# Attention sums into an ELU layer on one core: a later place for z in the head, and two 128-row stores at the end

## The chip, the cores and the metric

The kernel runs on one core of one Trainium2 chip. The metric is the device time of one execution in microseconds (us); the kernel before takes 267.29 us (median of 3 runs, 267.2 to 267.3). Less is better. Engines are named as in the profile: PE is TensorE (PEld its weight loads), DVE is VectorE, ACT is ScalarE, POOL is GpSimd, SP is SyncE, whose only work here is to issue transfers (DMAs); ACT can issue transfers too.

## The reference

What is computed, cut to what matters:

```python
batch, n_heads, seq, head_dim, r = 4, 4, 1088, 32, 8       # x: 4352 tokens x 128; w_in 128 x 2048, w_out 2048 x 128
def phi(x):                                   # 32 features -> 64
    a = einsum('rd,bhsd->bhsr', S1, x)
    b = einsum('rd,bhsd->bhsr', S2, x)
    return einsum('bhsi,bhsj->bhsij', a, b).reshape(..., r * r)
q_p, k_p = phi(q), phi(k)
kv  = einsum('bhsf,bhsd->bhfd', k_p, v)
z   = sum(k_p, axis=2)
num = einsum('bhsf,bhfd->bhsd', q_p, kv)
den = einsum('bhsf,bhf->bhs', q_p, z)[..., None] + 1e-06
x   = (num / den).transpose(0, 2, 1, 3).reshape(4352, 128)
h   = x @ w_in
g   = where(h > 0, h, exp(minimum(h, 0)) - 1)
out = g @ w_out
```

The arrays are given in 64-bit floats, so the weights are turned into 32-bit floats on the chip (the functions RA, RB and RC, some five instructions for each block of weights, most of them on DVE).

## The kernel before, in words

The sequence is cut into 68 half tiles of 64 tokens (17 for each of 4 batches); a token of batch b, place y and half tile t is row (b, y, t) of the output, so neighbouring rows of one half tile lie 17 output rows apart (`NT = 17`), and half tile t+2 lies two rows behind half tile t. Nine query groups `g` hold up to 8 half tiles each; the last, `g = 8`, holds four.

The order of work is written out by hand: the order of the calls is the order of each engine's queue, and engines wait for each other only where data asks for it. There are three stages.

**The head** (to about 22 us). For batch 0: DVE transposes the keys (`transp(kT, ...)`, L244), `KF(0)` multiplies them with the sketch matrices on PE (tile `abp`, L304) and ACT copies the result out of PSUM in two pieces (`abk`, L312). Two things are made of these key features:
- z, the sums for the denominator. `Z_first` gives PE 9 small products (`zps`, L382, 18 instructions), ACT copies their result (`zl`, L404), `Z` multiplies it with a mask matrix on PE (`zps`, L226, 4 instructions) and `Z_out` writes z into `SW` on DVE (L413). `q1z_first` multiplies the queries with it on PE (`zqp`, L491).
- the products of the features, `kp`: `KO_pool` makes the first four tiles of nine on POOL (L287), `KO_first(t0, t1)` the tiles t0 to t1 on DVE (L374, out of PSUM). `KA(0)` sums them with v on PE (`kv`, L391).

`q1_first` does for the queries what `KF` does for the keys (`abqp`, L479, copied by ACT to `abq`, L483); it needs the transposed queries (`qT`, L244). `q2_den` makes the quotient on DVE: `pw` (L566) from `abq` and `zqp`, then `den`, `an`, and `q2_out` the query features `qp` (L583). Behind it on DVE come the roundings of the first weights and the second query group; the first `mm2` (tile `o`, L226) follows them. `keep_warm(n, cols)` gives PE n products of cols columns whose result nobody reads (`idle`, L231).

**The middle.** For each group and each 256-wide block of w_in: `h` on PE, two ACT passes (L788, L790), one DVE pass (L796), and the second product on PE (`o`, or `pa` and `pb`, L727).

**The end.** The last group ends in `mm2_last`, which leaves two PSUM tiles of 128 tokens x 128 features, each of two half tiles (`ol`, i = 0 and 1; output half tiles 64+i in partitions 0 to 63 and 66+i in partitions 64 to 127). `fin_last` copies tile 0 by ACT and tile 1 by DVE (L840) and stores each tile as two transfers of 64 rows, one issued by SP and one by ACT (L843).

Of the kernel before, what the change touches and what calls it, by code (L numbers as in the profile page):

```python
# [22 lines left out]
def _ap(ap: bass.AP, free):  # L23
    return dataclasses.replace(ap, ap=[list(ap.ap[0])] + [list(x) for x in free])
# [3 lines left out]
def kernel(  # L28
# [21 lines left out]
    nc = tc.nc  # L50
# [8 lines left out]
    KT = (NT + 1) // 2  # L59
# [164 lines left out]
    def halves(dst, lhs, rhs, **kw):  # L224
        for u in range(2):
            nc.tensor.matmul(dst[64 * u:64 * u + 64], lhs[:, 64 * u:64 * u + 64], rhs, skip_group_check=True,  # L226
                             tile_position=(0, 64 * u), **kw)

    def keep_warm(n, cols=256):
        for i in range(n):  # L230
            nc.tensor.matmul(idle[:, :cols], some[:, :P], some[:, :cols], skip_group_check=True)  # L231
# [11 lines left out]
    def transp(dst, x, b, t0, t1):  # L243
        nc.vector.transpose(dst[b][:, t0:t1, :].rearrange("p t (a c) -> p c t a", c=2), hd[x, b][:, :, t0:t1, :])  # L244
# [124 lines left out]
    def KO_first(t0, t1):  # L369
        half, o = divmod(t0, 5)  # L370
        n = t1 - t0
        a_ = kf_ps[half][:, 64 * o:64 * (o + n)].rearrange("p (m x r) -> p m x r", x=2, r=R)[:, :, 1, :]
        b_ = feats[0][:, 0, t0:t1].rearrange("p t h r -> p (t h) r")
        nc.vector.tensor_mul(feats[0, half][:, o:o + n].rearrange("p t h i j -> p (t h) i j"),  # L374
                             _ap(a_, list(a_.ap[1:]) + [[0, R]]), _ap(b_, [[R, n * H], [0, R], [1, R]]))
# [3 lines left out]
    def z_tile(b, ps, i):  # L379
        c = 32 * (i % 4)  # L380
        ab = feats[b]
        nc.tensor.matmul(ps[c:c + 32, R * R:R * R + H * R], ab[:, 0, i].rearrange("p h r -> p (h r)"),  # L382
                         ab[:, 1, i].rearrange("p h r -> p (h r)"), start=(b == 0 and i < 4), stop=(i >= KT - 4),
                         skip_group_check=True, tile_position=(0, c))
# [17 lines left out]
    def ZC(b, ps):  # L402
        zl = work.tile([P, H * R], F32, name="zl", tag="zl")
        nc.scalar.copy(zl[:], ps[:, R * R:R * R + H * R])  # L404
        return zl

    def Z(b, ps, zl):

        halves(ps[:, 96:128], SXh[:], zl[:])

    def Z_out(b, ps):
        z = wzs[b] = SW[:, :, 2, :] if b == 0 else work.tile([FD, H, R], F32, name="wz", tag="wz")[:]
        nc.vector.tensor_mul(z, ps[:, 96:128].rearrange("p (h i) -> p h i", h=H), _ap(bmask[:], [[1, H], [0, R]]))  # L413
# [21 lines left out]
    def Z_first():  # L435
        ps = psum.tile([P, 512], F32, name="zps", tag="h", bufs=4)
        for i in range(KT):
            z_tile(0, ps, i)
        return ps, ZC(0, ps)

    def KS_first():
        kd = work.tile([P, 2, R * R], F32, name="kd", tag="kd", bufs=1)
# [18 lines left out]
    def half_tile(g, k):  # L461
        return divmod(8 * g + k, NT)
# [11 lines left out]
    def q1_first():  # L474
        p = psum.tile([P, 512], F32, name="abqp", tag="aux")
        for i in range(4):
            for u in range(2):
                b, t = half_tile(0, 2 * i + u)
                nc.tensor.matmul(p[64 * u:64 * u + 64, i * 64:i * 64 + 64], qT[b][:, t, :],  # L479
                                 Sab[:].rearrange("p h y -> p (h y)"),  # L480
                                 skip_group_check=True, tile_position=(0, 64 * u))
        abw[0] = work.tile([P, H * 4, 2 * R], F32, name="abq", tag="abq", bufs=1)
        nc.scalar.copy(abw[0][:].rearrange("p (h t) y -> p h t y", h=H),  # L483
                       p[:, :256].rearrange("p (t h y) -> p h t y", t=4, h=H))

    def q1z_first():
        p = psum.tile([P, 512], F32, name="zqp", tag="h", bufs=4)
        for i in range(4):
            for u in range(2):
                b, t = half_tile(0, 2 * i + u)  # L490
                nc.tensor.matmul(p[64 * u:64 * u + 64, i * 32:i * 32 + 32].rearrange("p (h r) -> p h r", h=H),  # L491
                                 qT[b][:, t, :], SW[:, :, 2, :], skip_group_check=True, tile_position=(0, 64 * u))
        return p[:, :128].rearrange("p (t h r) -> p h t r", t=4, h=H)
# [341 lines left out]
    def fin_last():  # L835
        g, n = NQ - 1, qn[NQ - 1]
        o = work.tile([P, 2, P], F32, name="ol", tag="ol", bufs=1)
        rows = out.rearrange("(b y t) f -> b y t f", b=B, t=NT)
        for i, copy in enumerate((nc.scalar.copy, nc.vector.tensor_copy)):
            copy(o[:, i, :], ops[g][i][:])  # L840
            for u, eng in enumerate((nc.sync, nc.scalar)):
                b, t = half_tile(g, u * n + i)
                eng.dma_start(rows[b, :, t, :], o[64 * u:64 * u + 64, i])  # L843


    for t0, t1 in ((0, 5), (KT, KT + 5), (5, KT), (KT + 5, NT)):
        transp(kT, "k", 0, t0, t1)
    KF(0)
    transp(qT, "q", 0, 0, 8)
    zps, zl = Z_first()  # L850
    q1_first()
    KO_pool()
    KO_first(4, 5)
    KO_first(5, 7)
    Z(0, zps, zl)
    Z_out(0, zps)
    KO_first(7, KT)
    keep_warm(1, 96)
    zq = q1z_first()
    RA(0)  # L860
    q2_den(0, zq)
# [132 lines left out]
    for n in range(2, N + 2):  # L994
        if n < N:
            g, cp = steps[n]
# [26 lines left out]
        g, cp = steps[n - 2]  # L1023
# [5 lines left out]
        elif n > 2:  # L1029
            mm2(g, cp, cp == 0, cp == NP - 1)  # L1030
            if cp == NP - 1:
                fin1(g)
    fin_last()


# [27 lines left out]
```

## Time and profile before

| | |
|---|---|
| median of 3 runs | 267.29 us (267.2 to 267.3) |
| the profiled execution, its own time | 267.2 us |
| its span, first to last instruction | 265.4 us |
| granted TensorE clock, mean | 0.998 |
| PE busy | 259.6 us (98%) |
| DVE busy | 187.5 us (71%) |
| ACT busy | 184.1 us (69%) |
| POOL busy | 159.9 us (60%) |
| mean traffic of the transfers | 51 GB/s |

The profile is of one execution. Between the span and that execution's own time lie 1.8 us which are not in the trace. In lines of instructions the first number is the start in us from the begin of the span, the second the time from the start of the first to the end of the last of the instructions that the line holds; "xN" is how many there are, and the bracket says how long the engine was idle before and for whom it waited. Times of DMA-issuing instructions (SPq, ACTq) are those of the issue; the data moves later.

### The profile page before, as it was taken

Reading aid. Unit: us, or ns where it says so; the run is one execution under the profiler, and the core shown is the slowest. Engines: PE = TensorE matmul, PEld = TensorE weight load, DVE = VectorE, ACT = ScalarE, POOL = GpSimd, SP = SyncE. Lnnn points to the kernel's source line nnn. Section 1 sums busy time; section 2 is a strip of 40 time slices with the busy share of each in tenths; the row PEclk is TensorE's granted clock in tenths of the full one; section 3 lists DMA queues with packets and bytes.
Section 4 is the critical chain, followed back from the end, with each engine's and each line's share of the span. In section 5 each row is a group of like instructions: output and inputs, shape, how many; then the busy total and the mean of one; then the engine's idle time right before and its main releaser. Section 6 shows DMA issues by size and latency. Waiting matters only on the chain.

```text
span 265.4 us, 7688 instructions
## 1 busy us (share of the span) xinstructions
PE 259.6 (98%) x3115; PEld 154.4 (58%) x3115; DVE 187.5 (71%) x347; ACT 184.1 (69%) x355; POOL 159.9 (60%) x233
## 2 busy tenths in 40 slices
PE   8999999999999999999999999999999999999994
PEld 6752323343334665667666666666766666666884
DVE  6899999996969796996557776654346444673652
ACT  2479978667567566785577777777777777777782
POOL 4400009104316985798859799898688888898300
PEclk9999999999999999999999999999999999999999
DMA  5999960020002200001100110001001100010011
GB/s 191 324 347 260 264 177 4 0 67 22 0 0 38 48 4 0 2 3 20 27 2 0 23 21 2 0 13 24 11 0 18 28 1 0 14 16 15 2 28 34
DMA packets 26418, 13.60 MB, mean 51 GB/s; under 512 B 19216, under 2 KB 24592, under 8 KB 26384
## 3 DMA queue, kind: packets, MB, share of 16 engines
q1 hardware_dynamic: 25792, 12.66, 18.7%
q8 instruction: 24, 0.39, 0.6%
q10 hardware_dynamic: 592, 0.46, 0.5%
q14 instruction: 10, 0.08, 0.1%
HBM read 10.88 MB, written 2.23 MB: 49 GB/s over the span
## 4 chain that ended last, share of the span: by engine, by line
PE 93%; DVE 5%; issue 1%; ACT 0%; DVEq 0%
PE h L226 43%; PE pb L727 16%; PE pa L727 12%; PE o L226 11%; PE ol L226 3%; PE kv L391 1%; PE idle L231 1%; PE h L645 1%; PE qps L645 1%; DVE qp L583 1%; PE kfps L323 1%; PE qps L539 1%; PE abp L304 1%; PE kv L226 1%; DVE raw L121 0%
## 5 line engine op out<-in xcount | busy, mean ns | idle before, releaser
L796 DVE SCALAR_TENSOR_TENSOR gg<-e,h 128x512 f32<-128x512 f32 (+1 forms) x144 | 92.2, 652 | 64.1 <-ACT e L790 62.8
L226 PE MATMUL h<-xg,W 128*64 128x512 f32 (+1 forms) x584 | 128.7, 563 | 0.0
L788 ACT ACTIVATE e<-h 128x512 f32<-128x512 f32 (+1 forms) x144 | 81.5, 566 | 50.4 <-PE h L226 47.9
L790 ACT ACTIVATE e<-e 128x512 f32<-128x512 f32 (+1 forms) x144 | 87.5, 607 | 4.4
L226 PEld LDWEIGHTS h<-xg,W 128*64 128x64 f32 x584 | 40.1, 137 | 47.4 <-issue 36.8
L707 POOL TENSOR_TENSOR tt<-gg 128x256 f32<-128x256 f32 x48 | 35.2, 733 | 16.3 <-DVE gg L796 15.9
L710 POOL TENSOR_TENSOR tt<-gg 128x256 f32<-128x256 f32 x48 | 35.4, 738 | 14.2 <-DVE gg L796 13.8
L712 POOL TENSOR_TENSOR tt<-gg,tt 128x256 f32<-128x256 f32 x48 | 36.6, 762 | 3.8
L711 POOL TENSOR_TENSOR tt<-tt,gg 128x256 f32<-128x256 f32 x48 | 35.2, 734 | 3.8
L727 PEld LDWEIGHTS pa<-gg,W 128*64 128x64 f32 x384 | 23.6, 137 | 22.7 <-issue 22.0
L226 PE MATMUL o<-gg,W 128*64 128x512 f32 x128 | 30.5, 597 | 0.4 <-DVE W L129 0.4
L727 PE MATMUL pa<-gg,W 128*64 128x128 f32 x384 | 29.5, 274 | 0.0
L727 PE MATMUL pb<-tt,SS 128*64 128x128 f32 x384 | 29.1, 273 | 0.0
L727 PEld LDWEIGHTS pb<-tt,SS 128*64 128x64 f32 x384 | 22.6, 137 | 0.0
L126 POOL TENSOR_TENSOR raw<-raw,tiny 128x512 f32<-128x512 f32 x1 | 1.0, 1046 | 29.7 <-DVE raw L121 29.7
L727 PE MATMUL pb<-gg,SS 128*64 128x128 f32 x192 | 18.7, 273 | 0.0
L727 PE MATMUL pb<-tt,W 128*64 128x128 f32 x192 | 18.7, 273 | 0.0
L727 PE MATMUL pa<-tt,SS 128*64 128x128 f32 x192 | 18.7, 273 | 0.0
L226 PEld LDWEIGHTS o<-gg,W 128*64 128x64 f32 x128 | 8.5, 136 | 16.2 <-issue 13.8
L727 PEld LDWEIGHTS pa<-tt,SS 128*64 128x64 f32 x192 | 12.1, 137 | 0.0
L727 PEld LDWEIGHTS pb<-tt,W 128*64 128x64 f32 x192 | 12.1, 137 | 0.0
L727 PEld LDWEIGHTS pb<-gg,SS 128*64 128x64 f32 x192 | 12.1, 137 | 0.0
(150 smaller groups left out, 243.8 us busy)
## 6 DMA issues: line engine op xcount, KB each, us to landing
raw<-in_moe_w_in_dram SPq DMA_DIRECT2D x8, 256.0 KB, 5.8
raw<-in_moe_w_out_dram SPq DMA_DIRECT2D x8, 256.0 KB, 6.0
hd_k<-in_k_dram SPq DMA_DIRECT2D x3, 544.0 KB, 7.6
hd_q<-in_q_dram SPq DMA_DIRECT2D x3, 544.0 KB, 3.2
v<-in_v_dram SPq DMA_DIRECT2D x4, 288.0 KB, 6.5
out_dram<-ob SPq DMA_DIRECT2D x72, 16.0 KB, 1.5
v<-in_v_dram SPq DMA_DIRECT2D x4, 256.0 KB, 7.5
out_dram<-ob SPq DMA_DIRECT2D x16, 32.0 KB, 1.7
```

Source lines behind the costliest of these rows:

```text
L226: nc.tensor.matmul(dst[64 * u:64 * u + 64], lhs[:, 64 * u:64 * u + 64], rhs, skip_group_check=True, tile_position=(0, 64 * u), **kw)
L231: nc.tensor.matmul(idle[:, :cols], some[:, :P], some[:, :cols], skip_group_check=True)
L304: nc.tensor.matmul(ps[i // 5][64 * u:64 * u + 64, 64 * (i % 5):64 * (i % 5) + 64], kT[b][:, u * KT + i, :], Sab[:].rearrange("p h y -> p ( ...
L645: nc.tensor.matmul(ps[w][s * r:s * r + s, 64 * k:64 * (k + m)], lhs, qpT[g, i][rows, o + 2 * k:o + 2 * (k + m), f, :], start=(f == 0 and j ...
L707: nc.gpsimd.tensor_tensor(t[:, 0], b12, b11, op=SUB)
L710: nc.gpsimd.tensor_tensor(t[:, 2], b22, b12, op=SUB)
L711: nc.gpsimd.tensor_tensor(t[:, 1], t[:, 2], b11, op=ADD)
L712: nc.gpsimd.tensor_tensor(t[:, 3], b21, t[:, 1], op=SUB)
L727: nc.tensor.matmul(bank[64 * u:64 * u + 64, P * col:P * col + P], lhs, rhs[:, u], start=(first and i in (0, 3)), stop=last, skip_group_che ...
L788: nc.scalar.activation(e, hs[g, cp][c][:, :n], RELU, scale=-1.0)
L790: nc.scalar.activation(e, e, EXP, scale=-1.0)
L796: nc.vector.scalar_tensor_tensor(gs[g, cp][:, c, :n], es[g, cp][:, c, :n], -1.0, hs[g, cp][c][:, :n], op0=ADD, op1=MAX)
```

## The change

Two places are changed. In the head, all of z's steps (the sums, ACT's copy, the mask product, `Z_out` and the filling product on PE) become one function that is called behind `q1_first`, `KO_pool` and all of `KO_first`; `KO_first` for the tiles 5 to 8 becomes one instruction in place of two; the filling product has 160 columns in place of 96. At the end, each of the two last tiles is stored by one transfer of 128 rows, the first issued by ACT, the second by SP.

```diff
@@ Z_first
         for i in range(KT):
             z_tile(0, ps, i)
-        return ps, ZC(0, ps)
+        zl = ZC(0, ps)
+        Z(0, ps, zl)
+        Z_out(0, ps)
+        keep_warm(1, 160)
@@ fin_last
-        for i, copy in enumerate((nc.scalar.copy, nc.vector.tensor_copy)):
+        for i, (copy, eng) in enumerate(((nc.scalar.copy, nc.scalar), (nc.vector.tensor_copy, nc.sync))):
             copy(o[:, i, :], ops[g][i][:])
-            for u, eng in enumerate((nc.sync, nc.scalar)):
-                b, t = half_tile(g, u * n + i)
-                eng.dma_start(rows[b, :, t, :], o[64 * u:64 * u + 64, i])
+            b, t = half_tile(g, i)
+            eng.dma_start(rows[b, :, t:t + n + 1:n, :].rearrange("y u f -> u y f"), o[:, i])
@@ the head's calls
     KF(0)
     transp(qT, "q", 0, 0, 8)
-    zps, zl = Z_first()
     q1_first()
     KO_pool()
     KO_first(4, 5)
-    KO_first(5, 7)
-    Z(0, zps, zl)
-    Z_out(0, zps)
-    KO_first(7, KT)
-    keep_warm(1, 96)
+    KO_first(5, KT)
+    Z_first()
     zq = q1z_first()
```

In the new store `n` is 2. The side in SBUF is 128 partitions of 128 elements. The side in DRAM is written as (u, y, f): two groups u of 64 rows y of 128 elements f; u steps by 2 output rows, y by 17.

## The prediction

> **What bounds the kernel now.** I read the page first, then the chain of waits, the timeline of the head and of the end, and the traffic of single transfers. The page:
>
> ```profile
> span 265.4 us, 7688 instructions
> PE 259.6 (98%) x3115; PEld 154.4 (58%) x3115; DVE 187.5 (71%) x347; ACT 184.1 (69%) x355; POOL 159.9 (60%) x233
> GB/s 191 324 347 260 264 177 4 0 67 22 0 0 38 48 4 0 2 3 20 27 2 0 23 21 2 0 13 24 11 0 18 28 1 0 14 16 15 2 28 34
> ```
>
> PE is busy for 98%, but that is a mean over stages. The chain of waits (start, length, what) shows who carries the head:
>
> ```profile
> 8.07 0.61 PE abqp L479 x16
> 8.69 0.11 PE zps L226 x4
> ...
> 8.90 0.19 DVE SW L413
> 9.09 0.60 DVE kp L374
> ...
> 9.92 0.30 DVE pw L566
> ...
> 11.26 1.29 DVE qp L583 x2
> ...
> 21.30 0.44 DVE W L129
> 21.73 0.04 issue
> 21.78 1.94 PE o L226 x8
> ```
>
> From 8.90 to 21.73 every step is one of DVE, with gaps of issue alone. From 21.78 on PE runs to 261.91 with no pause that counts. So DVE time lost or won ahead of 21.73 reaches the end in full: PE's `o` waits for DVE's last weight rounding, and nothing between them has slack. DVE has one idle stretch after 7.5 us, ahead of SW (timeline: start, length, what, and in brackets the idle time before it):
>
> ```profile
> 7.47 1.00 DVE L374 TENSOR_TENSOR kp<-abp,abk 128x256 f32<-128x256 f32 x2
> ...
> 8.14 0.19 ACT L404 COPY zl<-zps 128x32 f32<-128x32 f32 x1 [0.39 <-PE zps L382]
> ...
> 8.74 0.37 ACT L483 COPY abq<-abqp 128x256 f32<-128x256 f32 x1 [0.41 <-PE abqp L479]
> 8.90 0.19 DVE L413 TENSOR_TENSOR SW<-zps,bmask 128x32 f32<-128x32 f32 x1 [0.42 <-PE zps L226]
> ```
>
> The end is a row of steps behind the last matmul: copy, issue, packets, landing.
>
> ```profile
> 261.79 1.20 SPq L843 DMA_DIRECT2D out_dram<-ol  x2
> 261.79 1.19 ACTq L843 DMA_DIRECT2D out_dram<-ol  x2
> 261.93 0.29 DVE L840 COPY ol<-ol 128x128 f32<-128x128 f32 x1 [1.04 <-PE ol L226]
> ```
>
> Each issue takes 0.55; the second pair leaves at 262.44. By the traffic of this window the first packet starts 1.21 after the first issue (263.00) and the last ends at 264.05; 1.37 more pass to the end of the span (265.42).
>
> **The head, step by step.** Removed: one start of an instruction (two pieces of `KO_first` are joined). Moved: z's steps, past `q1_first` on PE, past the `abq` copy on ACT, past POOL's products (z gives POOL no instruction there, and no transfer moves) and past one `KO_first` piece on DVE. New times:
> - `q1_first` now waits for `qT` alone. That ends at 7.55 (6.84 + 0.71); DVE to PE takes 0.05 (SW ends 9.09, `zqp` starts 9.14). It takes 0.69: 7.60 to 8.29.
> - ACT copies `abq` first: 8.34 to 8.71 (0.05 behind PE as now, 0.37 long).
> - PE does z's 18 pieces behind `q1_first`. The parts of 8 and 10 pieces took 0.27 and 0.31, mostly drain, so 18 end at about 8.6, under the `abq` copy: nothing.
> - `zl` 0.19 on ACT: 8.71 to 8.90. It was under `q1_first` before; now it is on the path.
> - mask product: 0.05 hand-over and 0.26: ends 9.21. To DVE 0.12 (8.78 to 8.90 now): SW 9.33 to 9.52.
> - `zqp`: 0.05 + 0.66: ends 10.23; to DVE 0.12: `pw` at 10.35.
>
> `pw` starts at 9.92 now: **+0.43 us**. On DVE the joined `KO_first` (0.68 + 0.60 now; joining saves some 0.08) ends by 9.1, ahead of SW, and the rounding RA (0.28) lies between SW and `pw`; both fill waiting, so neither counts. Behind the waiting SW on DVE stand RA, and behind that ACT's RB; behind the later `pw` stands the whole DVE chain to 21.73. KA on PE starts 0.4 later too and its result is needed no earlier than before, relative to DVE. The filling product costs nothing while SW's wait covers it: 64 more columns, twice, at 0.86 ns (256 columns in 0.22 at 11.53) are 0.11; that puts its end about 0.1 ahead of `zqp`; with that cover gone it costs up to 0.1. Bounds: 0.3 (`zl` overlapping the copy ahead of it by 0.1, as ACT's neighbours elsewhere do) to 0.6 (z's pieces 0.1 later, the filling product uncovered). What is late next is PE's `o` at 22.2, and by it all the rest.
>
> **The end, step by step.** Two issues of 0.55 fall away, one on each queue. SP no longer has a first store: its only one goes when DVE's copy ends (262.22, so 262.25 in place of 262.44), a gain of 0.19. The trace has no 128-row issue of this form: 0.33 (a 128-row weight load on SP) to 0.74 (a load on ACT); I take 0.55, nearest in form. Nothing is queued behind it but the end of the program.
>
> What counts is how the packets spread. The traffic from 1.68 to 1.82, where the two 8-row loads of the sketch matrices pass (queue q1 is SP's, q10 ACT's; packets, MB, share of 16 engines):
>
> ```profile
> q10 hardware_dynamic: 16, 0.00, 9.0%
> q1 hardware_dynamic: 16, 0.00, 8.6%
> ```
>
> from 252.6 to 253.0, one store of 128 runs over 32 partitions:
>
> ```profile
> q1 hardware_dynamic: 144, 0.02, 26.2%
> ```
>
> and from 262.5 on, the last four stores:
>
> ```profile
> q10 hardware_dynamic: 160, 0.07, 10.0%
> q1 hardware_dynamic: 160, 0.07, 8.1%
> ```
>
> A load of 8 rows makes 16 packets: 8 of data and 8 of 4 bytes. A store of 64 rows makes 80 (64 + 16; each queue has two), the one of the middle 144 (128 + 16). So each engine that a transfer uses adds one small packet, and an outermost count of 8 gets 8 engines where 64 or 32 get 16. And the two 8-row loads, from SP and ACT, share their engines: packet by packet, ACT's start some 20 ns behind SP's (1.703 and 1.723, 1.705 and 1.726, 1.707 and 1.731).
>
> The new store counts 128 outermost in SBUF, but 2 in DRAM: u steps 2 rows, y 17, so they don't fold. I take the smaller count to decide, as 8 did: 2 engines, 64 rows each, the same 2 for both stores. That is 128 packets of 512 B on each of them; now each of 16 gets 16 (8 for each pair of stores). The page's best slice, 347 GB/s, is 21.7 per engine: 23.6 ns a packet (the stores' own packets follow each other by 23.5 and are recorded with 27). 128 x 23.6 ns = 3.02 us from ACT's first packet at 263.00: 266.02 in place of 264.05, **+1.97 us**. SP's earlier issue is then worth nothing, since its packets join a queue. Bounds: 16 engines, -0.2 (SP's 0.19; with the issue at 0.33, -0.4); at 30 ns a packet (the stores' engine time, 52.3% of 16 x 0.5 us in the window from 263.6, less the small ones, over 128) +2.85. The nearest row is the 8-row load, the only one with few outer rows, so I take +1.97.
>
> The Trainium skill speaks both ways. "DMA: Bandwidth & Descriptors", section on rules for kernel authors, says that two transfers to disjoint partition halves share the same engines anyway and advises one 128-partition transfer; by this alone the end would be about -0.2. The same page, section "Why a DMA increments its semaphore by 16 and not by 1", says that the engines used are the largest number up to 16 that divides the slowest dimension of both sides: 2 here; by it the end is +1.97. The packets of the 8-row loads fit the second; no row here has two sides with different outer counts.
>
> **Sum.** 267.2 (the profiled execution: span 265.4 and 1.8 around it) + 0.43 + 1.97 = **269.6 us**. The median is 267.29, 0.1 above that execution, within this rounding.
>
> **The rivals.**
> 1. *The rows spread over 16 engines* (the SBUF side's 128 decides). Then packets take 0.42 as now, the end gives 0.2 back, and only the head is left: 267.2 + 0.43 - 0.2 = 267.4, not slower by what can be told. For it: all stores in the trace use 16. Against: all of these have 32 or more outer rows on both sides. It decides from 8 engines on: both stores are then 32 packets on each engine, 0.75, done by 263.9, ahead of now; on 4 engines 64 packets take 1.51, to 264.51, and the sum is 268.1.
> 2. *Two engines for each store, but not the same two.* SP's packets start at 263.46 (262.25 + 1.21) and take 64 x 23.6 = 1.51: 264.97, +0.92, so 268.55. Against it: the pairwise packets of the 8-row loads.
> 3. *Two engines that write slower than the mean rate*, at 30 ns or more a packet: 267.2 + 0.43 + 2.85 = 270.5. For it: some stores' packets took 40 to 50 ns when SP and ACT wrote together.
> A gain in the head would need SW ahead of 8.90, but `zl` can't start before 8.6 and SW comes 0.6 behind it.
>
> **How the numbers follow.** Forecast 0.70 (own range 269.1 to 270.2: the head's 0.3 to 0.6, 23.6 to 27 ns a packet, the first packet up to 0.2 earlier with a short issue), rival 1 0.18, rival 2 0.06, rival 3 0.06. The forecast and rivals 2 and 3 leave 0.18 and their own tails out, so the range reaches down to rival 1's middle, 267.4, and up to rival 3's, 270.6. Within 0.2% (0.53 us, about what a measurement of this kernel can tell from no change): most of rival 1, 0.14. Slower: the rest, 0.84. Faster by more: 0.02.
>
> **What would show it.** Right: SW near 9.3 after a wait for `zps`, `pw` near 10.35 after a second wait, for `zqp`, and PE's first `o` near 22.2; 130 packets for each last store (128 + 2), traffic at some 43 GB/s for about 3 us, and a span near 267.8. Wrong in the end: 144 packets in a burst of 0.4 us. Wrong in the head: `o` at 21.8 or earlier.

## The result, and the profile after

The changed kernel takes 270.37 us (median of 6 runs, 269.95 to 270.84); the kernel before took 267.51 us in the runs beside it (6 runs, 267.2 to 268.47). The ratio is 1.0103, 95% interval 1.0081 to 1.0124: slower by 1%. The forecast was 269.6 us, in a range from 267.4 to 270.6; 270.37 lies near the upper end of it. The profiled execution took 270.53 us with a span of 268.7; before it was 267.2 with 265.4.

The chain of waits of the changed kernel, in its head (start, length, what):

```profile
2.07 5.25 DMA hd_q<-in_q_dram
7.32 0.02 issue
7.34 0.72 DVE qT L244
8.06 0.14 issue
8.20 0.70 PE abqp L482 x16
8.92 0.37 ACT abq L486
9.29 0.13 ACT zl L404
9.43 0.14 issue
9.56 0.31 PE zps L226 x4
9.87 0.47 PE idle L231 x2
10.34 0.61 PE zqp L494 x16
10.95 0.02 issue
10.98 0.30 DVE pw L569
...
22.38 0.44 DVE W L129
22.82 0.04 issue
22.86 1.94 PE o L226 x8
```

Read it from below. PE's first `o` starts at 22.86 where it started at 21.78: 1.08 us later. `pw` is 1.06 later (10.98 for 9.92), so the DVE chain between them hands the delay on whole. And the chain now runs back through the queries (`abqp`, `abq`, `qT`) to the load of q; before, it ran back through z's sums to the key features. The waits of DVE in the first 23 us (in total, times, longest) say the same:

```profile
DVE qT L244 <- DMA hd_q<-in_q_dram: 0.9, 1, 0.9
...
DVE pw L569 <- PE zqp L494: 0.6, 1, 0.6
DVE SW L413 <- PE zps L226: 0.5, 1, 0.5
```

and in the profile before:

```profile
DVE SW L413 <- PE zps L226: 0.4, 1, 0.4
...
DVE qT L244 <- DMA hd_q<-in_q_dram: 0.2, 1, 0.2
```

There are two waits for z's chain, SW's and `pw`'s, where there was one of 0.4. The wait for the q load was 0.2 and is 0.9: q landed later in this execution, by 0.50 at the end of `qT` (8.05 for 7.55). Its transfers were issued at the same times as before, to 0.02 us, and none of the moved steps runs ahead of it.

The end, by the timeline and by the traffic from 262.5 us on (40 slices of GB/s; then packets, MB and share of 16 engines for ACT's and SP's queue):

```profile
262.87 0.66 ACTq L845 DMA_DIRECT2D out_dram<-ol  x1
263.01 0.29 DVE L843 COPY ol<-ol 128x128 f32<-128x128 f32 x1 [1.04 <-PE ol L226]
263.33 0.63 SPq L845 DMA_DIRECT2D out_dram<-ol  x1
```

```profile
GB/s 0 0 0 0 0 0 0 0 0 0 13 20 30 40 46 43 26 40 26 43 43 46 40 43 46 43 43 43 43 43 46 40 0 0 0 0 0 0 0 0
...
q10 hardware_dynamic: 130, 0.07, 4.0%
q1 hardware_dynamic: 130, 0.07, 3.5%
```

The same row of the profile before, also from 262.5 us on:

```profile
GB/s 0 0 0 0 0 0 28 92 233 297 184 64 7 0 0 28 113 170 262 234 92 7 0 0 0 0 0 0 0 0 0 0 0 0 0 0 0 0 0 0
```

130 packets for each store are 128 rows and 2 small ones: two engines. The traffic is a long shelf at 43 GB/s, the rate of two engines, in place of two short bursts. Its packets start from 264.16 to 267.48 (3.32 us); before, they started from 263.00 to 264.05. From the end of DVE's copy to the end of the span it is 5.40 us in place of 3.20. So the span's 3.28 us are 1.08 in the head and 2.20 at the end.

### The profile page after: what moved, and what is told of

Read it like the earlier page. It is cut to its first block, busy times and chain, and to the rows that moved or that the text cites. A ratio compares the mean times of both kernels' runs of the same rounds, so it can differ in the third digit from the quotient of the medians.

```text
span 268.7 us, 7682 instructions
## 1 busy us (share of the span) xinstructions
PE 259.3 (97%) x3115; PEld 154.1 (57%) x3115; DVE 187.3 (70%) x346; ACT 184.0 (68%) x355; POOL 159.8 (59%) x233
## 4 chain that ended last, share of the span: by engine, by line
PE 90%; DVE 4%; DMA 2%; issue 1%; ACTq 0%; ACT 0%; DVEq 0%
PE h L226 42%; PE pb L730 16%; PE pa L730 12%; PE o L226 11%; PE ol L226 3%; DMA hd_q<-in_q_dram 2%; PE kv L391 1%; PE h L648 1%; PE qps L648 1%; DVE qp L586 1%; PE kfps L323 1%; PE qps L542 1%; PE kv L226 1%; DVE qT L244 1%; DVE raw L121 0%
```

## The experiments

Eight kernels were run, each timed beside the kernel before. Two theories were to be told apart for each place: at the end, that the outermost count of the DRAM side sets the number of engines, or that a store of 128 rows is slow in itself; in the head, that z's chain behind the queries costs the time, or the new order on DVE, or the late load of q.

The landmarks of all profiles, in us. "End" is from the end of DVE's copy of tile 1 to the end of the span. "Engines" is the number of small packets of each wide store (of each 64-row store for before, head_only and z_early).

| kernel | `qT` ends | first `zps` | `pw` | `pw` - `qT` | `pw` - `zps` | first `o` | end | engines |
|---|---|---|---|---|---|---|---|---|
| before | 7.55 | 7.39 | 9.92 | 2.37 | 2.53 | 21.78 | 3.20 | 16 |
| changed | 8.05 | 8.82 | 10.98 | 2.92 | 2.16 | 22.86 | 5.40 | 2 |
| tail_only | 7.48 | 8.12 | 10.64 | 3.17 | 2.53 | 22.53 | 5.40 | 2 |
| head_only | 7.81 | 8.57 | 10.73 | 2.92 | 2.16 | 22.60 | 3.17 | 16 |
| rows16 | 7.29 | 8.05 | 10.21 | 2.92 | 2.16 | 22.09 | 2.91 | 16 |
| one_wide | 7.31 | 7.50 | 10.03 | 2.72 | 2.53 | 21.91 | 4.06 | 2 |
| rows4 | 8.08 | 8.84 | 11.00 | 2.92 | 2.16 | 22.87 | 3.95 | 4 |
| best1 | 7.58 | 8.20 | 10.73 | 3.15 | 2.53 | 22.62 | 2.91 | 16 |
| by_half | 7.46 | 8.08 | 10.60 | 3.14 | 2.53 | 22.51 | 3.32 | 16 |
| z_early | 7.52 | 8.14 | 10.70 | 3.18 | 2.56 | 22.56 | 3.20 | 16 |

**tail_only: the new stores alone.** The kernel before with `fin_last` of the change.

> The head is that of before; only the two last tiles are stored as in the change (128 rows each, ACT and SP). Theory (two engines carry all rows): in the profiles the stretch from the end of DVE's last copy to the end of the span went from 3.20 us (262.22 to 265.42) to 5.4 us (263.30 to 268.7), so this kernel is 2.2 us above before; 130 packets per store, traffic near 43 GB/s for 3.0 to 3.3 us; PE's first o at 21.8 as before. Rival (the end is slow only behind the later head, or the head carries most of the loss): under 1.5 us above before.

Measured: 269.84 us against 267.80, ratio 1.0084 (1.0062 to 1.0106), so 2.0 us by the medians and 1.7 to 2.8 by the interval. The end is 5.40, the same as in the changed kernel, and each store has 130 packets. The end alone carries most of the loss. The expected 21.8 for `o` was a miss: it came at 22.53 with the old head. That is the start of the key features, not the stores, as the head's part below shows.

**head_only: z's new place alone.** The changed kernel with `fin_last` of before.

> The end is that of before; only z's steps are moved as in the change. Theory (z's chain copy, mask product, SW, zqp now stands alone behind q1_first): pw starts 2.9 us behind the end of the qT transposition (10.98 against 8.06 in the changed kernel's profile) in place of 2.4 us (9.92 against 7.55), so 0.55 us above before, less or more only by where the q load lands; DVE waits about 0.5 for SW and 0.6 for pw. Rival (the q load, which landed 0.5 us later in the changed kernel's profile, lands later because of the change): 1.1 us above before and qT again after 7.3 us. Second rival (the shift is swallowed by PE's later work): under 0.2 us above before.

Measured: 268.07 us against 267.80, ratio 1.0012 (0.9997 to 1.0028): 0.3 us by the medians, from nothing to 0.75 by the interval, so by time alone not settled. The landmarks are exact, though. DVE's timeline:

```profile
7.09 0.71 DVE L244 STREAM_TRANSPOSE qT<-hd_q 128x512 f32<-128x512 f32 x1 [0.37 <-DMA hd_q<-in_q_dram]
...
9.73 0.19 DVE L413 TENSOR_TENSOR SW<-zps,bmask 128x32 f32<-128x32 f32 x1 [0.48 <-PE zps L226]
...
10.73 0.29 DVE L569 TENSOR_TENSOR pw<-abq,zqp 128x128 f32<-128x128 f32 x1 [0.60 <-PE zqp L494]
```

The two waits are there, and `pw` comes 2.92 behind the end of `qT`, as in all four kernels with this head. The q load was neither as early as in the profile of before nor as late as in that of the change, and in rows16, with the same head, `qT` ended at 7.29: so the new head does not delay it in every execution, and the 1.1 us of that rival did not come. A tendency is not excluded: in the other three kernels with the new head `qT` ended at 7.81 to 8.08, later than in all six with the old order on PE (7.31 to 7.58).

**rows16: the same wide stores, 64 outermost.** The last group's columns are written in another order, so that partition 2y+u holds place y of group u; then the DRAM side counts (y, u). The diff is cut to the expressions that change, each behind the name of its function.

```diff
-  q5_out:    x[:, :2 * n].rearrange("p (k w s) -> p w k s", w=2, s=64)[:, w]
+             x[:, :2 * n].rearrange("p (k s w) -> p w k s", w=2, s=64)[:, w]
-  fin_last:  eng.dma_start(rows[b, :, t:t + n + 1:n, :].rearrange("y u f -> u y f"), o[:, i])
+             eng.dma_start(rows[b, :, t:t + n + 1:n, :], o[:, i])
```

> As the changed kernel, but the last group's tokens are laid out so that neighbouring partitions hold the two groups u of one y: the DRAM side of each 128-row store then counts (y, u), 64 outermost, in place of (u, y), 2 outermost. Same bytes, same rows, same engines that issue. Theory (the outer count sets the number of engines): 144 packets per store in a burst of some 0.5 us, the end 0 to 0.3 us shorter than before, the whole 0.3 to 0.6 us above before by its head. Rival (a single store of 128 rows and 64 KB is slow in itself, whatever its outer count): 2.7 us above before, as the changed kernel.

Measured: 267.72 us against 267.80, ratio 1.0002 (0.9987 to 1.0018), so nothing by the medians and 0.5 us at most by the interval, where 0.3 to 0.6 was expected for the head: a miss, to which the head's part below comes back. The traffic from 262 us on:

```profile
GB/s 0 0 0 0 0 0 0 0 113 259 32 123 259 22 0 0 0 0 0 0 0 0 0 0 0 0 0 0 0 0 0 0 0 0 0 0 0 0 0 0
...
q10 hardware_dynamic: 144, 0.07, 3.5%
q1 hardware_dynamic: 144, 0.07, 3.5%
```

Same rows, same bytes, same issuing engines; only the order of the two outer counts differs. 144 packets each, two bursts, and the end is 2.91: 2.49 less than with 2 outermost, and 0.29 less than with four stores. That a store of 128 rows is slow in itself falls.

**rows4: 4 outermost.** Again by the order of the last group's columns (cut in the same way, new lines only): each store covers 32 places of all four half tiles, DRAM side (4, 32).

```diff
+  q5_out:    x[:, :2 * n].rearrange("p (i w k l) -> p w k i l", i=2, w=2, k=2)[:, w]
+  fin_last:  eng.dma_start(rows[b, 32 * i:32 * i + 32, t:t + 2 * n, :].rearrange("y u f -> u y f"), o[:, i])
```

> As the changed kernel, but the last group's tokens are laid out so that each of the two last stores covers 32 places y of all four half tiles, and its DRAM side counts (4 half tiles, 32 places): outermost 4 in place of 2, same bytes and packets. Theory (the engines used are as many as divide both outermost counts): 4 engines, 132 packets per store, 64 packets on each engine: 1.5 us at 23.6 ns, up to 1.8 with the slow start seen with two; from the end of DVE's copy to the end of the span 3.6 to 3.9 us (5.40 with two engines, 2.91 with sixteen), so 1.0 to 1.3 above before with its head. Rival (any outermost count that isn't a multiple of 16 falls to the same slow path): 5.4 us behind the copy, as the changed kernel.

Measured: 268.91 us against 267.73, ratio 1.0036 (1.0021 to 1.0052): 1.2 us by the medians, where 1.0 to 1.3 was expected. From 263 us on:

```profile
GB/s 0 0 0 0 0 0 0 0 0 0 0 38 33 67 81 76 95 86 86 72 57 43 95 76 95 86 81 52 0 0 0 0 0 0 0 0 0 0 0 0
...
q10 hardware_dynamic: 132, 0.07, 5.6%
q1 hardware_dynamic: 132, 0.07, 5.5%
```

132 packets are 4 engines, the shelf is at 86 GB/s, twice that of two engines, and the end is 3.95, 0.05 above what was expected at most. It isn't all or nothing: with 2, 4 and 64 outermost, against 128 on the SBUF side, the stores used 2, 4 and 16 engines.

**one_wide: one of the two stores.** The kernel before, tile 0 by one 128-row store, tile 1 by two of 64 rows.

```diff
+        nc.scalar.copy(o[:, 0, :], ops[g][0][:])
         ...
+        nc.scalar.dma_start(rows[b, :, t:t + n + 1:n, :].rearrange("y u f -> u y f"), o[:, 0])
         ...                       # tile 1 as before
```

> The head is that of before; tile 0 is stored by one 128-row transfer on ACT, tile 1 by two of 64 rows as before. Theory (engine time adds up on two engines): 64 packets of 23.6 ns from 263.0 are 1.51, then four and four of tile 1's packets on the same engines 0.19: last packet near 264.7 in place of 264.05, 0.65 us above before. Rival (each 128-row transfer costs the same extra): half of what both cost, 1.1 us above before. Rival (the loss is only the second one waiting for the first): under 0.3 us above before.

Measured: 268.61 us against 267.80, ratio 1.0034 (1.0019 to 1.0048), 0.8 us by the medians; the end is 4.06, 0.87 longer than before. That is between the first theory (0.65) and the first rival (1.1); the last packet ended at 265.04, where it was to be near 264.7 for a first packet at 263.0. The first packet came at 263.20. Of the other 0.14, some 0.05 was lost by 263.35, in the wide store's first packets, and most of the rest between 264.14 and 264.51, while tile 1's packets passed. The issues (KB, us to landing) show the queueing:

```profile
out_dram<-ol SPq DMA_DIRECT2D x1, 32.0 KB, 2.8
out_dram<-ol ACTq DMA_DIRECT2D x1, 32.0 KB, 2.9
```

Tile 1's stores use 16 engines and land after 2.8 and 2.9 in place of 2.1 and 1.9, since a few of their rows share two engines with the wide store. SP's first packets start at 263.83, but its last eight only from 264.65 on, and then each of the two engines takes packets of the two queues in turn. The traffic from 264.645 to 264.835:

```profile
q1 hardware_dynamic: 8, 0.00, 7.1%
q10 hardware_dynamic: 8, 0.00, 7.1%
```

This is what the theory says and the others don't, but the size was not hit; by time alone (0.5 to 1.3 us) the first rival is not excluded.

**best1: the better of both.** The head of before with the stores of rows16.

> The head of before, and at the end the 128-row stores with 64 places outermost (16 engines). Theory: 2.9 us from the end of DVE's copy to the end of the span in place of 3.2, so 0.3 us faster than before. Rival (the gain of one store for each tile is lost in the head's spread or given back by ACT's later issue): same as before within 0.1 us.

Measured: 267.27 us against 267.73, ratio 0.9987 (0.9975 to 1.0000): 0.3 us faster by the ratio, with the interval just at no change. The end is 2.91 for 3.20, as expected. It has the lowest ratio of the ten, by little.

**by_half: two stores of 64 rows of 1 KB.** The head of before; both copies first, then each half of the partitions in one store with both tiles. Of the diff, the new lines:

```diff
+        for u, eng in enumerate((nc.sync, nc.scalar)):
+            b, t = half_tile(g, u * n)
+            eng.dma_start(rows[b, :, t:t + n, :], o[64 * u:64 * u + 64])
```

> The head of before; each of the two last stores covers 64 partitions and both tiles, so 64 rows of 1 KB outermost in place of 128 rows of 512 B, one issued by SP and one by ACT, both behind the second copy. Theory: issue right behind the copy on both queues, 16 engines, 160 packets in all with their small ones, some 2.9 us from the end of DVE's copy to the end of the span: 0.2 to 0.3 us faster than before. Rival (the early start of the first store counts): both stores at once collide and the stretch stays at 3.2 us.

Measured: 267.52 us against 267.73, ratio 0.9996 (0.9983 to 1.0010), the end 3.32: the theory (2.9) missed, and its rival (3.2) is nearer, though too low as well. Both issues leave within 0.02 us of each other (263.01 and 263.03), but the landings differ:

```profile
out_dram<-ol SPq DMA_DIRECT2D x1, 64.0 KB, 2.0
out_dram<-ol ACTq DMA_DIRECT2D x1, 64.0 KB, 2.3
```

ACT's packets begin 0.28 behind SP's (264.50 and 264.22). Why is open; in before and z_early, whose first two stores are also issued together, the first packets lie only 0.06 apart, in head_only 0.15. In rows16 and best1, whose stores are issued 0.46 apart, each starts its packets some 1.3 behind its issue.

**z_early: the order on DVE alone.** The end of before, z's sums and `zl` directly behind the key features as before, but mask product, SW and the filling product behind all of `KO_first`.

```diff
-    KO_first(5, 7)
+    KO_first(5, KT)
     Z(0, zps, zl)
     Z_out(0, zps)
-    KO_first(7, KT)
-    keep_warm(1, 96)
+    keep_warm(1, 160)
```

> The end of before. Of the head's change only the DVE part: z's sums and their copy stay directly behind the key features, but the mask product, SW and the filling product of 160 columns come behind all of KO_first, joined to one instruction. Theory (of the head's loss most is z's chain standing alone behind the queries): SW waits for KO_first only, so pw starts 2.65 to 2.7 us behind the first z piece in place of 2.53, 0.15 us above before. Rival (the order on DVE is the loss): pw 3.0 us or more behind it, 0.5 us above before.

Measured: 267.88 us against 267.73, ratio 1.0004 (0.9992 to 1.0016). `pw` comes 2.56 behind the first z piece, where 2.65 to 2.7 was expected and 2.53 is the old order. DVE's timeline:

```profile
8.12 1.64 DVE L374 TENSOR_TENSOR kp<-abp,abk 128x256 f32<-128x256 f32 x2 [0.60 <-ACT abk L312]
9.67 0.18 DVE L413 TENSOR_TENSOR SW<-zps,bmask 128x32 f32<-128x32 f32 x1
```

SW follows `KO_first` with no wait. So the order on DVE costs 0.03 at these arrivals, and what is left for the rest of the head's cost is z's chain behind the queries.

**What the head's landmarks say together.** With the old order `pw` starts 2.53 us behind the first z piece, with `qT` at 7.31 to 7.58 (five of five). With the new order it starts 2.92 behind the end of `qT` (four of four). The change thus exchanged the input that binds: the key features for the queries. Its price in one execution is (`qT` + 2.92) less (first `zps` of the old order + 2.53). With the landmarks of the profile before, that is 7.55 + 2.92 - 7.39 - 2.53 = 0.55. With those of tail_only the sum would be 7.48 + 2.92 - 8.12 - 2.53 = -0.25, but a gain does not follow: z_early, whose inputs came as in tail_only (`qT` 7.52, first `zps` 8.14), shows SW behind `KO_first` until 9.67, and the changed kernel has the same `KO_first` ahead of SW. By that row `pw` comes at least 2.56 behind the first z piece, a price of 0.03, an estimate. The key features were late in tail_only since the matmuls ahead of them ran at half rate until about 6.7 us. The filling products at 5.2 us (two pieces of 224 columns) show it, tail_only first and one_wide second:

```profile
5.26 0.95 PE L231 MATMUL idle<-some 128*128 128x224 f32 x2
```

```profile
5.21 0.54 PE L231 MATMUL idle<-some 128*128 128x224 f32 x2
```

So the head's cost changes from execution to execution, by these rows from about nothing to 0.55, which fits the small mean of head_only. Three pairs of kernels differ in the head alone: head_only and before, rows16 and best1, changed and tail_only. Their ratios differ by 0.0012, 0.0015 and 0.0019, or 0.3, 0.4 and 0.5 us. Each is within its noise, and the last two pairs were timed in different rounds, but all three lie on the same side and near the forecast's 0.43. How the price spreads over many executions was not measured.

## Why the prediction was right, point by point

- **DVE's time passes to the end in full.** Right. From `pw` to the first `o` it is 11.86 to 11.90 us in all ten profiles, and PE from there on takes the same 240.1 us in both kernels (to 261.88 and 262.96).
- **The head, +0.43.** The mechanism held: two waits on DVE, `zl` on the path, KO and RA in the waiting. From the end of `qT`, where the forecast began, `pw` was put at 2.80 and came at 2.92, so the term is 0.55 in place of 0.43 at the same arrivals. The mis-sized step is the hand-over to PE, taken as 0.05 from SW to `zqp`: from `qT` to `abqp` it was 0.15, from `zl` to the mask product 0.14. The filling product stands on the chain above, so its cover is gone: `zqp` starts 0.10 behind SW. ACT's `zl` overlapping the copy ahead of it gave 0.06 back, and the way from `zqp` to `pw` 0.07 (0.05 for 0.12). What the forecast did not see is that its 0.43 was the price at one arrival of the inputs: it took the profile's `qT` and `zps` as fixed. In the profile after, `qT` alone is 0.50 later, so SW (9.98), `pw` (10.98) and `o` (22.86) all came some 0.6 later than the signs that the prediction named.
- **The end, +1.97.** Two engines, the same two for both stores: right, and 2.20 in size. The first packet came 1.29 behind the issue for 1.21, with the issue at 0.66 for 0.55 (0.08); the packets took 3.32 for 3.02 (0.30). Of this, 0.14 was lost by 264.5, where some packets took 52 to 81 ns, and 0.14 between 265.0 and 265.4 (41 to 107 ns); otherwise each engine started one every 23.5 ns. The way from the last packet's start to the end of the span was 1.22 for 1.37 (-0.15).
- **Rival 1** (16 engines) is out by the 130 packets; its price, some 0.2 of gain at the end, is what rows16 measured (0.29). For 4 engines the prediction had 0.46 more at the end (264.51 for 264.05); rows4 took 0.75 more. **Rival 2** (other engines for the second store) is out: SP's first packet started at 265.94, when ACT's last row was on its way (its packet ended at 265.97), 1.4 us after its queue was ready by the 1.21 of the forecast (263.33 + 1.21). **Rival 3** (slower engines) holds only for the two stretches named above, some 0.4 us each.
- **The sum.** 270.37 is 0.77 above 269.6. Of this 0.31 is the level (the kernel before had 267.51 in these runs; the sum starts from 267.2), 0.23 the end and 0.12 the head; the remaining 0.1 fits the scatter of the head's inputs and is not shown. 270.37 is above the forecast's own range (269.1 to 270.2) and nearer to rival 3's 270.5; it lies in the stated range because that reached up to rival 3. The mechanism is the forecast's all the same, as the packets show, and with the level of these runs its own range would end at 270.5.
- **The page's two rules.** The Trainium skill's "DMA: Bandwidth & Descriptors", section "Why a DMA increments its semaphore by 16 and not by 1", was the one that bound: 2, 4 and 16 engines for outer counts of 2, 4 and 64 against 128. The advice in its rules for kernel authors, one 128-partition transfer for two halves, holds too, but only when the first rule is kept: -0.29 us with 64 outermost, +2.20 with 2.

## What to carry to other kernels

Before two stores are joined into one, look at the outermost count on each side: where one is small, a few engines carry all rows. All counts tried here are powers of two, so the runs can't tell the smaller count from the largest common divisor of the rule above. Count the small packets in the traffic, one for each engine used, and mind that the order of tokens may be open to choice some steps earlier: in rows16 and rows4 an ACT copy writes it, and the two copies took 0.43 to 0.45 us for 0.44 before. When a step is moved on a path to the first full use of an engine, ask which input binds the path before and after: its price holds for one arrival of the inputs only.

## What the runs showed of the hardware that was not expected

- Two stores on the same two engines from two queues did not share them evenly: in the changed kernel SP's packets started when ACT's were all but through (265.94 and 265.97). In one_wide SP's few rows on the shared engines were let in at 264.65, after 56 or 57 of the wide store's 64 packets on each, and from then on the two queues alternated packet by packet.
- Two 64-row stores issued 0.02 us apart, on SP and on ACT, started their packets 0.28 us apart in by_half, and 0.06 apart in before.
- PE's matmuls in the first microseconds ran at half rate in four executions until some 6.5 to 6.9 us (224 columns twice in 0.95 us in place of 0.54; in tail_only `abp` starts every 107 ns up to 6.74 and every 58 or so behind it), while the row of the granted clock reads 1.00 there; with the old head `pw` came up to 0.8 us later in such executions (10.73 and 9.92).
- PE's `abqp` started 0.15 us behind `qT` in all four kernels with the new head, and the mask product 0.14 behind `zl`, where the prediction had taken 0.05 from another place. A long wait of PE is not what sets it: in the changed kernel it had waited 1.04 us, in rows16 its work ended as `abqp` began (7.44). What does was not tried.
